# Another opening for a Fourier filter with a two-layer product behind it: where x, the constants and the weights are loaded, and in which order the first steps stand

## The chip, the cores and the metric

The kernel runs on one core of a Trainium2 chip. The metric is the device time of one execution in microseconds (us). Five engines work side by side, each through its own queue of instructions in order: TensorE (PE; its weight loads are listed as PEld), VectorE (DVE), ScalarE (ACT), GpSimd (POOL) and SyncE (SP). DMA transfers are asked for by SP (hardware_dynamic queue q1 in the profile) and by POOL (software_dynamic queue q0); the transfers of both run on the same 16 DMA engines.

## The reference

x has 8 sequences of 3008 tokens with 256 channels, in fp32. Each sequence is filtered by multiplying its Fourier transform with a given complex filter, and each token of the result goes through two matrices with a leaky ReLU between them:

```python
X = np.fft.rfft(x, axis=1)                       # x: (8, 3008, 256)
Y = X * (filt_r + 1j * filt_i)[None, :, :]       # filters: (1505, 256)
y = np.fft.irfft(Y, n=x.shape[1], axis=1).astype(np.float32)
h = y.reshape(24064, 256) @ w_in                 # w_in: (256, 2048)
g = np.maximum(0.01 * h, h)
out = (g @ w_out).astype(np.float32)             # w_out: (2048, 256)
```

## The kernel before

**Tiles and stages.** A sequence is seen as 94 x 32 tokens (N1 = 94 on the partitions, N2 = 32 rows in `x_sb`), and its transform as four small products in fp16. Stage 1 (`s1`) multiplies the 94 side with `fwd1`, a part of `small_sb`. A turn of the data brings the 32 side onto the partitions. Stage 2 (`s2`) multiplies each of 24 columns with its own constant matrix in `f2_sb`; the result is multiplied with the filter in `fa_sb`. Stage `sa` (`inv2r`, `inv2i`) goes back along the 32 side, a second turn follows, and stage `sb` multiplies with `i1_sb` and leaves the filtered sequence in `yt`. From `yt` the two-layer part takes chunks of 512 tokens, 47 of them: `moe1` (L511) multiplies with `w_in_sb`, ACT applies the leaky ReLU (L516), and the second product uses `w_out_sb`, plainly in the first three chunks (L636) and by Strassen's seven products from the fourth on (L575).

**The first sequence** has a way of its own, since nothing can hide it: its turns are DVE transposes (`t1`, `t2`, four each; 0 and 1 belong to the first half of the channels, 2 and 3 to the second) between the buffers `big[0]`, `big[1]` and `big[2]`, not trips through DRAM. The order in which its steps are issued is written out by hand in the string FIRST. Each word calls a function that issues instructions to one engine, and each engine takes its instructions in that order:

- `s1p n0 n b`: PE, stage 1 for rows n0 to n0+n of x into PSUM bank b; `s1e n0 n e`: its eviction by ACT (A) or DVE (D).
- `s2p half c n i b`: PE, stage 2 for n columns from c, i = 0 or 1 for two forms of the constant; `s2d`: DVE multiplies the result with the filter; `s2a` and `s2m`: ACT copies it out of PSUM, four columns at a time, and POOL multiplies it.
- `sap half c b`: PE, stage `sa`, which needs both products of its four columns; `sae`: its eviction by ACT.
- `sbp dt h b`: PE, stage `sb` for half dt of the channels and block h of 376 tokens; `sbe`: its eviction to `yt`. The first chunk of `moe1` needs blocks 0 and 1 of both halves.
- `warm n`: n matmuls on PE with no use for their result.
- `x`, `w_out` (POOL), `f2`, `i1` (SP, each behind a tiny memset on DVE): loads that are issued at that place. `x` loads the second sequence into `x_sb`.
- `xc n0 n e`: rounds rows of x that were loaded in fp32 to fp16.

Ahead of FIRST the first loads are issued: by SP `small_sb` and six of the 32 rows of x in fp32 into the later `big[1]`; by POOL, which casts to fp16 on the way, the other rows in parts of 10, 10 and 6, the first third of `f2_sb`, eight loads of the filters (two half channels, real and imaginary, each in two loads) and `w_in_sb`. POOL's issues wait for earlier ones: the ninth is issued when the first has landed, the tenth when the second has.

**After FIRST** everything is ordered by a planner: each step has a due time in slots (8 to a chunk), and PE alternates between `moe1`, the second product and the stages of the next sequence. Stage 1 of the second sequence (L250) starts in the first chunk, one group of two rows of x after the other; groups 0 to 7 use the first half of `x_sb`, groups 8 to 15 the second. The last stores go out by SP and ACT both.

Of the kernel before, what the change touches and what calls it, by code (L numbers as in the profile page):

```python
# [11 lines left out]
P = 128  # L12
FP16 = mybir.dt.float16
FP32 = mybir.dt.float32
# [5 lines left out]
N1, N2 = 94, 32  # L20
NC = 24
Q = 32
R1 = 96
FP = 3
# [51 lines left out]
def kernel(  # L76
# [9 lines left out]
    nc = tc.nc  # L86
    B, N, D = x.shape
# [33 lines left out]
    f2_d = nc.inline_tensor(f2_np, name="fwd2_const")  # L121
# [6 lines left out]
    f2_sb = cpool.tile([P, NC, P], FP16, name="f2_sb")  # L128
# [5 lines left out]
    w_out_sb = cpool.tile([P, NCT, D], FP16, name="w_out_sb")  # L134
    wt_sb = cpool.tile([P, 4, NCH, P], FP16, name="wt_sb")
    x_sb = cpool.tile([P, N2, D], FP16, name="x_sb")
    big = [cpool.tile([P, Q * D], FP16, name=f"big{i}") for i in range(3)]
# [50 lines left out]
    def x_load(b, n0=0, nn=N2, d0=0, dn=D):  # L188

        for lo, cnt in ((0, R1),) if b + 1 < B else ((0, 64), (64, N1 - 64)):  # L190
            nc.gpsimd.dma_start(
                x_sb[lo : lo + cnt, ds(n0, nn), ds(d0, dn)],
                bass.AP(tensor=x.tensor, offset=x.offset + (b * N + lo * N2 + n0) * D + d0,
                        ap=[[N2 * D, cnt], [D, nn], [1, dn]]))

    def filt_load(lo, src, d0, dn):

        for q, first, sgn in ((lo, 0, 1), (lo + Q, N1, -1)):
            nc.gpsimd.dma_start(
                fa_sb[q : q + Q, :, ds(d0, dn)],  # L200
                bass.AP(tensor=src.tensor, offset=src.offset + first * D + d0,
                        ap=[[N1 * D, N2 // 2], [sgn * NC * D, 2], [sgn * D, NC], [1, dn]]))

    EARLY = 6
    x_early = big[1][:].bitcast(FP32)[:, : EARLY * D].rearrange("p (n d) -> p n d", n=EARLY)
    nc.sync.dma_start(small_sb[:], small_d.ap())
    nc.sync.dma_start(x_early[:R1], bass.AP(tensor=x.tensor, offset=x.offset, ap=[[N2 * D, R1], [D, EARLY], [1, D]]))
    for n0, nn in ((6, 10), (16, 10), (26, 6)):  # L210
        x_load(0, n0, nn)
    nc.gpsimd.dma_start(f2_sb[:, : NC // FP, :], f2_d.ap()[0])
    for hf in range(2):

        filt_load(0, filt_r, hf * DH, DH)
        filt_load(64, filt_i, hf * DH, DH)
    nc.gpsimd.dma_start(w_in_sb[:], moe_w_in.rearrange("(dt p) c -> p dt c", p=P))
    idle = cpool.tile([P, CH], FP16, name="idle")
    nc.vector.memset(idle[:], 0.0)
# [136 lines left out]
    engine = {"A": act, "D": dve}  # L356
# [91 lines left out]
        nc.vector.memset(i1_sb[:, 0, 0:2], 0.0)  # L448
        nc.sync.dma_start(i1_sb[:], i1_d.ap())

    def load_f2():
        nc.vector.memset(f2_sb[:, NC // FP, 0:2], 0.0)
        nc.sync.dma_start(f2_sb[:, NC // FP :, :].rearrange("p (i c) m -> p i (c m)", i=FP - 1),
                          f2_d.ap()[1:].rearrange("i p c m -> p i (c m)"))

    def load_x(half):
        x_load(1, half * N2 // 2, N2 // 2)
        issued.add(("x", 1, 0))

    def load_w_out():  # L460
        nc.gpsimd.dma_start(w_out_sb[:], moe_w_out.rearrange("(ct p) d -> p ct d", p=P))

    def round_x(n0, n, e):
        engine[e](x_sb[:N1, ds(n0, n), :], x_early[:N1, ds(n0, n), :])

    FIRST = """
        xc 0 4 A, xc 4 2 D, warm 18, s1p 0 0 4 b3, s1p 0 4 2 b0, warm 3, s1p 0 14 2 b1, s1e 0 4 2 D,
        s1e 0 0 4 A, s1p 0 10 4 b4, s1e 0 10 4 A, s1p 0 6 4 b3, s1e 0 14 2 D, warm 4, s1p 0 20 4 b4,
        s1e 0 6 4 D, s1p 0 16 4 b3, s1e 0 16 4 A, s1p 0 26 2 b2, s1p 0 24 2 b0, s1e 0 24 2 A, f2, s1e 0 20 4 D,
        s1p 0 28 2 b1, s1p 0 30 2 b4, s1e 0 26 2 D, s1e 0 30 2 A, s1e 0 28 2 D, t1 0, t1 1, warm 14,  # L470
        s2p 0 0 4 0 b3, s2p 0 0 4 1 b2, warm 2, s2p 0 8 4 1 b0, s2a 0 0 4 0, s2a 0 0 4 1, t1 3,
        s2p 0 12 4 1 b4, t1 2, s2d 0 8 4 1, s2p 0 12 4 0 b1, s2p 0 16 8 0 b3, x 0, x 1, s2m 0 0 4 0,
        s2m 0 0 4 1, s2d 0 16 8 0, s2a 0 12 4 1, s2p 0 8 4 0 b2, s2p 1 16 8 0 b4, s2p 0 4 4 1 b0, s2a 0 12 4 0,
        s2d 0 8 4 0, s2a 1 16 8 0, s2p 0 4 4 0 b1, s2p 1 16 8 1 b3, s2d 0 4 4 0, s2a 1 20 8 0, sap 0 8 b2,
        s2d 0 4 4 1, s2a 1 16 8 1, s2a 1 20 8 1, s2m 0 12 4 0, s2p 0 16 8 1 b4, sap 0 0 b1, s2p 1 0 8 1 b3,
        s2m 0 12 4 1, sap 0 12 b0, s2m 1 20 8 0, sae 0 8 A, s2d 0 16 8 1, sae 0 0 A, s2p 1 8 8 1 b4,
        sap 0 4 b2, i1, s2d 1 0 8 1, sap 0 16 b1, sae 0 12 A, s2p 1 8 8 0 b3, sap 0 20 b0, s2d 1 8 8 1,
        s2m 1 20 8 1, sae 0 4 A, s2d 1 8 8 0, s2p 1 0 8 0 b4, sae 0 16 A, sap 1 20 b2, s2d 1 0 8 0,
        sap 1 12 b1, sae 0 20 A, sap 1 8 b0, s2m 1 16 8 0, sae 1 20 A, s2m 1 16 8 1, w_out, sae 1 12 A,
        sae 1 8 A, sap 1 16 b3, sae 1 16 A, sap 1 4 b2, t2 1, sae 1 4 A, sap 1 0 b4, t2 0, sae 1 0 A, warm 4,  # L480
        sbp 0 1 b1, sbp 0 4 b0, sbp 0 0 b3, sbp 0 3 b2, t2 3, sbe 0 1 A, sbe 0 4 A, sbe 0 0 A, sbp 0 2 b4,
        sbp 0 7 b1, sbp 0 6 b0, t2 2, sbe 0 2 A, sbe 0 7 A, sbp 0 5 b3, sbp 1 0 b4, sbp 1 1 b1, sbe 0 6 A,
        sbe 0 5 A, sbe 1 1 A, sbe 0 3 D, sbe 1 0 D
    """
    steps = dict(s1p=s1p, s1e=s1e, t1=t1, s2p=s2p, s2d=s2d, s2a=s2a, s2m=s2m, sap=sap, sae=sae, t2=t2,
                 sbp=sbp, sbe=sbe, i1=load_i1, f2=load_f2, x=load_x, w_out=load_w_out,
                 xc=round_x, warm=keep_warm)
    for step in FIRST.split(","):
        what, *args = step.split()
        steps[what](*(int(v) if v.isdigit() else v for v in args))  # L490
# [184 lines left out]
    for b in range(1, B):  # L675
        z = 47 * (b - 4) if b > 4 else 0
        p = PLANS[min(b, 4) - 1]
# [18 lines left out]
    while queue:  # L696
        time, n, stage, b, g, f = heapq.heappop(queue)
# [62 lines left out]
```

## Time and profile before

| | |
|---|---|
| time, median of 3 runs (lowest, highest) | 756.67 us (755.65, 757.60) |
| the profiled execution | 756.67 us, of which the span from first to last instruction is 754.9 |
| PE busy | 738.9 us, 98% of the span |
| DVE, ACT, POOL busy | 67%, 74%, 22% |
| DMA | 113.64 MB, mean 151 GB/s |
| granted PE clock, mean | 0.996 |

The page lists busy times of the engines, the span in 40 slices, the DMA queues, the chain of work that ended last, and the costliest groups of instructions. Rows of the timeline have start, length, engine, line, operation, what is written and read, and in brackets how long the engine had been idle and who ended that. Times count from the first instruction. Sizes in DMA views are those of the data as written: x counts half of what is read.

### The profile page before, as it was taken

Reading aid. Unit: us, or ns where it says so; the run is one execution under the profiler, and the core shown is the slowest. Engines: PE = TensorE matmul, PEld = TensorE weight load, DVE = VectorE, ACT = ScalarE, POOL = GpSimd, SP = SyncE. Lnnn points to the kernel's source line nnn. Section 1 sums busy time; section 2 is a strip of 40 time slices with the busy share of each in tenths; the row PEclk is TensorE's granted clock in tenths of the full one; section 3 lists DMA queues with packets and bytes.
Section 4 is the critical chain, followed back from the end, with each engine's and each line's share of the span. In section 5 each row is a group of like instructions: output and inputs, shape, how many; then the busy total and the mean of one; then the engine's idle time right before and its main releaser. Section 6 shows DMA issues by size and latency. Waiting matters only on the chain.

```text
span 754.9 us, 19393 instructions
## 1 busy us (share of the span) xinstructions
PE 738.9 (98%) x8017; PEld 529.2 (70%) x8017; DVE 502.2 (67%) x686; ACT 559.8 (74%) x755; POOL 166.5 (22%) x168
## 2 busy tenths in 40 slices
PE   8799999999999999999999999999999999999997
PEld 3446667776777777877778777787777777777775
DVE  5777555677776776667667766776677676465565
ACT  4675787888887787787778777877777777777662
POOL 5502430332222222222233222212212210000000
PEclk9999999999999999999999999999999999999999
DMA  9996798887876567565676566444554333111011
GB/s 203 227 199 164 176 215 219 212 187 197 223 194 162 135 188 211 140 155 144 178 191 164 142 183 168 137 141 120 140 164 122 106 101 104 57 54 54 29 51 63
DMA packets 119672, 113.64 MB, mean 151 GB/s; under 512 B 16336, under 2 KB 92752, under 8 KB 119392
## 3 DMA queue, kind: packets, MB, share of 16 engines
q1 hardware_dynamic: 104543, 95.95, 43.2%
q0 software_dynamic: 14752, 16.19, 15.7%
q8 instruction: 62, 1.02, 0.6%
q10 hardware_dynamic: 289, 0.26, 0.1%
q14 instruction: 26, 0.21, 0.1%
HBM read 57.51 MB, written 50.33 MB: 143 GB/s over the span
## 4 chain that ended last, share of the span: by engine, by line
PE 91%; DMA 5%; DVE 2%; ACT 1%; POOL 1%; issue 0%; SPq 0%; DVEq 0%; ACTq 0%
PE ph L511 41%; PE po_ps L575 18%; PE pf L575 18%; PE pf L250 3%; PE pf L342 3%; PE pf L321 2%; PE pf L299 2%; DMA i_sb<-inv_const 1%; PE po_ps L636 1%; PE pf L636 1%; DMA f_sb<-fwd_const 1%; DMA dz<-big 1%; DMA big<-in_x_dram 1%; POOL y_b_g L314 1%; DMA p_b_g<-p_b_g 1%; PE pf L433 0%
## 5 line engine op out<-in xcount | busy, mean ns | idle before, releaser
L516 ACT ACTIVATE gt_c<-ph 128x1024 f16<-128x1024 f32 x376 | 385.7, 1026 | 135.2 <-PE ph L511 124.5
L511 PE MATMUL ph<-yt,w_in_sb 128*128 128x512 f16 (+7 forms) x1728 | 447.3, 351 | 0.2
L575 PEld LDWEIGHTS <-gt_c 128*128 128x128 f16 x2800 | 202.2, 98 | 91.2 <-issue 0.2
L314 POOL TENSOR_TENSOR y_b_g<-p_b_g,p_b_g 128x512 f16<-128x512 f32 x84 | 118.8, 1416 | 416.4 <-DMA p_b_g<-p_b_g 198.2
L575 PEld LDWEIGHTS <-big 128*128 128x128 f16 x2128 | 151.2, 98 | 61.6 <-issue 0.2
L511 PEld LDWEIGHTS <-w_in_sb 128*128 128x128 f16 x1728 | 137.5, 98 | 20.9 <-issue 1.5
L308 DVE TENSOR_TENSOR p_b_g<-pf,fb_sb 128x512 f32<-128x512 f32 x78 | 53.7, 688 | 32.6 <-PE pf L299 14.7
L575 PE MATMUL po_ps<-wt_sb,gt_c 128*128 128x128 f16 x704 | 70.0, 219 | 0.0
L575 PE MATMUL pf<-wt_sb,gt_c 128*128 128x128 f16 x688 | 68.4, 219 | 0.0
L575 PE MATMUL pf<-w_out_sb,gt_c 128*128 128x128 f16 x720 | 67.9, 219 | 0.0
L332 ACT CAST yt<-pf 128x376 f16<-128x376 f32 x120 | 56.3, 471 | 15.5 <-PE pf L342 8.0
L575 PE MATMUL po_ps<-wt_sb,big 128*128 128x128 f16 x720 | 67.4, 219 | 0.1
L575 PE MATMUL pf<-wt_sb,big 128*128 128x128 f16 x704 | 67.2, 219 | 0.0
L253 ACT CAST big<-pf 128x512 f16<-128x512 f32 x100 | 58.2, 588 | 11.9 <-PE pf L250 10.1
L575 PE MATMUL po_ps<-w_out_sb,gt_c 128*128 128x128 f16 x688 | 66.0, 219 | 0.0
L311 DVE TENSOR_TENSOR p_b_g<-pf,fa_sb 128x512 f32<-128x512 f32 x84 | 57.2, 682 | 1.4 <-POOL y_b_g L314 1.3
L548 DVE TENSOR_TENSOR big<-gt_c 128x2048 f16<-128x2048 f16 (+1 forms) x46 | 57.5, 1250 | 0.1
L548 DVE TENSOR_TENSOR gt_c<-gt_c 128x2048 f16<-128x2048 f16 x43 | 55.5, 1291 | 1.0
L548 DVE TENSOR_TENSOR big<-gt_c,big 128x2048 f16<-128x2048 f16 (+1 forms) x45 | 55.2, 1226 | 0.0
L548 DVE TENSOR_TENSOR big<-big,gt_c 128x2048 f16<-128x2048 f16 (+1 forms) x45 | 55.0, 1222 | 0.1
L323 ACT CAST big<-pf 128x512 f16<-128x512 f32 x84 | 49.0, 584 | 5.8 <-PE pf L321 4.0
L250 PE MATMUL pf<-x_sb,small_sb 94*128 94x512 f16 x112 | 42.7, 381 | 0.9 <-DVE big L253 0.9
(88 smaller groups left out, 619.7 us busy)
## 6 DMA issues: line engine op xcount, KB each, us to landing
dz<-big SPq DMA_DIRECT2D x98, 256.0 KB
p_b_g<-p_b_g SPq DMA_DIRECT2D x156, 128.0 KB
out_dram<-ost_c_h SPq DMA_DIRECT2D x119, 128.0 KB
big<-dz SPq DMA_DIRECT2D x42, 256.0 KB
big<-dz SPq DMA_DIRECT2D x56, 192.0 KB
x_sb<-in_x_dram POOLq DMA_DIRECT2D x40, 192.0 KB, 4.5
x_sb<-in_x_dram POOLq DMA_DIRECT2D x2, 768.0 KB, 18.8
w_in_sb<-in_moe_w_in_dram POOLq DMA_DIRECT2D x1, 1024.0 KB, 13.4
```

The lines of the kernel that those rows point to most:

```text
L250: nc.tensor.matmul(ps, fwd1[:N1], x_sb[:N1, ds(2 * g, 2), :], start=True, stop=True)
L253: copy(st[:, ds(2 * (g % 2), 2), :], ps)
L308: nc.vector.tensor_tensor(p2[:], ps, fb, AL.mult)
L311: nc.vector.tensor_tensor(p1[:], ps, fa, AL.mult)
L314: ("y", b, g), lambda: nc.gpsimd.tensor_tensor(y1[:], p1[:], p3[:], AL.add)))
L323: nc.scalar.copy(st2[h % 4][:, ds(2 * (g % 2), 2), :], ps)
L332: copy(yv, ps.rearrange("p c a -> p a c"))
L342: nc.tensor.matmul(ps[:, j, :], z2[h % 4][:K4, j, ts(dt, P)], i1_sb[:K4, 4 * h + j, :], start=True, stop=True)
L511: nc.tensor.matmul(ph[:, j, ds(t - ci * CH, e - t)], w_in_sb[:, dt, ts(ct, P)], yt[:, dt, ds(t % N, e - t)], start=(dt == 0), stop=(dt == ...
L516: nc.scalar.activation(gts[ci][:, ds(2 * g, 2), :], ph, AF.Lrelu)
L548: nc.vector.tensor_tensor(*(v[:, ds(c0, n)] for v in (o, i0, i1)), op)
L575: nc.tensor.matmul(po[:, t], a()[:, c, ts(t, P)], w[:, c, :], start=(c == 0), stop=(c == NCH - 1))
```

## The change

All rows of the first sequence of x are loaded by POOL's queue with the cast, in parts of 10, 10, 8 and 4; the fp32 load and the rounding steps `xc` are gone. The thirds of `f2_sb` are all loaded ahead of FIRST: the second and the first by SP right after `small_sb`, the last by POOL between the two halves of the filters; the step `f2` is gone. `x` now issues one half of the second sequence, `w_out_sb` and the other half, all three together on POOL; `w_out` is no step of its own. FIRST is another order of the same kinds of steps: `i1` comes earlier, `x` later, among POOL's products; the split of products between DVE and POOL, the PSUM banks and the warm matmuls differ in places.

```diff
--- before.py
+++ after.py
@@ -202,18 +202,18 @@
                         ap=[[N1 * D, N2 // 2], [sgn * NC * D, 2], [sgn * D, NC], [1, dn]]))
 
 
-
-    EARLY = 6
-    x_early = big[1][:].bitcast(FP32)[:, : EARLY * D].rearrange("p (n d) -> p n d", n=EARLY)
     nc.sync.dma_start(small_sb[:], small_d.ap())
-    nc.sync.dma_start(x_early[:R1], bass.AP(tensor=x.tensor, offset=x.offset, ap=[[N2 * D, R1], [D, EARLY], [1, D]]))
-    for n0, nn in ((6, 10), (16, 10), (26, 6)):
+    for i in (1, 0):
+        nc.sync.dma_start(f2_sb[:, ts(i, NC // FP), :], f2_d.ap()[i])
+    first_parts = ((0, 10), (10, 10), (20, 8), (28, 4))
+    for n0, nn in first_parts:
         x_load(0, n0, nn)
-    nc.gpsimd.dma_start(f2_sb[:, : NC // FP, :], f2_d.ap()[0])
     for hf in range(2):
 
         filt_load(0, filt_r, hf * DH, DH)
         filt_load(64, filt_i, hf * DH, DH)
+        if hf == 0:
+            nc.gpsimd.dma_start(f2_sb[:, ts(2, NC // FP), :], f2_d.ap()[2])
     nc.gpsimd.dma_start(w_in_sb[:], moe_w_in.rearrange("(dt p) c -> p dt c", p=P))
     idle = cpool.tile([P, CH], FP16, name="idle")
     nc.vector.memset(idle[:], 0.0)
@@ -448,43 +448,34 @@
         nc.vector.memset(i1_sb[:, 0, 0:2], 0.0)
         nc.sync.dma_start(i1_sb[:], i1_d.ap())
 
-    def load_f2():
-        nc.vector.memset(f2_sb[:, NC // FP, 0:2], 0.0)
-        nc.sync.dma_start(f2_sb[:, NC // FP :, :].rearrange("p (i c) m -> p i (c m)", i=FP - 1),
-                          f2_d.ap()[1:].rearrange("i p c m -> p i (c m)"))
-
-    def load_x(half):
-        x_load(1, half * N2 // 2, N2 // 2)
+    def load_x():
+
+        x_load(1, 0, N2 // 2)
+        nc.gpsimd.dma_start(w_out_sb[:], moe_w_out.rearrange("(ct p) d -> p ct d", p=P))
+        x_load(1, N2 // 2, N2 // 2)
         issued.add(("x", 1, 0))
 
-    def load_w_out():
-        nc.gpsimd.dma_start(w_out_sb[:], moe_w_out.rearrange("(ct p) d -> p ct d", p=P))
-
-    def round_x(n0, n, e):
-        engine[e](x_sb[:N1, ds(n0, n), :], x_early[:N1, ds(n0, n), :])
-
     FIRST = """
-        xc 0 4 A, xc 4 2 D, warm 18, s1p 0 0 4 b3, s1p 0 4 2 b0, warm 3, s1p 0 14 2 b1, s1e 0 4 2 D,
-        s1e 0 0 4 A, s1p 0 10 4 b4, s1e 0 10 4 A, s1p 0 6 4 b3, s1e 0 14 2 D, warm 4, s1p 0 20 4 b4,
-        s1e 0 6 4 D, s1p 0 16 4 b3, s1e 0 16 4 A, s1p 0 26 2 b2, s1p 0 24 2 b0, s1e 0 24 2 A, f2, s1e 0 20 4 D,
-        s1p 0 28 2 b1, s1p 0 30 2 b4, s1e 0 26 2 D, s1e 0 30 2 A, s1e 0 28 2 D, t1 0, t1 1, warm 14,
-        s2p 0 0 4 0 b3, s2p 0 0 4 1 b2, warm 2, s2p 0 8 4 1 b0, s2a 0 0 4 0, s2a 0 0 4 1, t1 3,
-        s2p 0 12 4 1 b4, t1 2, s2d 0 8 4 1, s2p 0 12 4 0 b1, s2p 0 16 8 0 b3, x 0, x 1, s2m 0 0 4 0,
-        s2m 0 0 4 1, s2d 0 16 8 0, s2a 0 12 4 1, s2p 0 8 4 0 b2, s2p 1 16 8 0 b4, s2p 0 4 4 1 b0, s2a 0 12 4 0,
-        s2d 0 8 4 0, s2a 1 16 8 0, s2p 0 4 4 0 b1, s2p 1 16 8 1 b3, s2d 0 4 4 0, s2a 1 20 8 0, sap 0 8 b2,
-        s2d 0 4 4 1, s2a 1 16 8 1, s2a 1 20 8 1, s2m 0 12 4 0, s2p 0 16 8 1 b4, sap 0 0 b1, s2p 1 0 8 1 b3,
-        s2m 0 12 4 1, sap 0 12 b0, s2m 1 20 8 0, sae 0 8 A, s2d 0 16 8 1, sae 0 0 A, s2p 1 8 8 1 b4,
-        sap 0 4 b2, i1, s2d 1 0 8 1, sap 0 16 b1, sae 0 12 A, s2p 1 8 8 0 b3, sap 0 20 b0, s2d 1 8 8 1,
-        s2m 1 20 8 1, sae 0 4 A, s2d 1 8 8 0, s2p 1 0 8 0 b4, sae 0 16 A, sap 1 20 b2, s2d 1 0 8 0,
-        sap 1 12 b1, sae 0 20 A, sap 1 8 b0, s2m 1 16 8 0, sae 1 20 A, s2m 1 16 8 1, w_out, sae 1 12 A,
-        sae 1 8 A, sap 1 16 b3, sae 1 16 A, sap 1 4 b2, t2 1, sae 1 4 A, sap 1 0 b4, t2 0, sae 1 0 A, warm 4,
-        sbp 0 1 b1, sbp 0 4 b0, sbp 0 0 b3, sbp 0 3 b2, t2 3, sbe 0 1 A, sbe 0 4 A, sbe 0 0 A, sbp 0 2 b4,
-        sbp 0 7 b1, sbp 0 6 b0, t2 2, sbe 0 2 A, sbe 0 7 A, sbp 0 5 b3, sbp 1 0 b4, sbp 1 1 b1, sbe 0 6 A,
-        sbe 0 5 A, sbe 1 1 A, sbe 0 3 D, sbe 1 0 D
+        warm 18, s1p 0 0 2 b0, s1e 0 0 2 A, s1p 0 2 4 b3, s1p 0 6 4 b4, s1e 0 2 4 D, warm 4, s1p 0 16 4 b3,
+        s1e 0 16 4 D, s1p 0 10 2 b1, s1e 0 6 4 A, s1p 0 12 4 b4, s1e 0 10 2 A, warm 2, s1p 0 24 2 b2,
+        s1e 0 12 4 A, s1e 0 24 2 D, s1p 0 20 4 b3, s1e 0 20 4 A, s1p 0 26 2 b0, s1p 0 28 2 b1,
+        s1p 0 30 2 b2, s1e 0 26 2 D, s1e 0 28 2 A, s1e 0 30 2 D, t1 1, t1 0, warm 14, s2p 0 0 4 0 b0,
+        s2p 0 0 4 1 b1, s2p 0 16 4 0 b2, t1 2, t1 3, s2a 0 0 4 0, s2m 0 0 4 0, s2a 0 0 4 1, s2p 0 16 4 1 b0,
+        s2p 0 8 8 0 b4, s2p 0 8 8 1 b3, s2a 0 16 4 0, s2m 0 16 4 0, s2a 0 16 4 1, s2m 0 16 4 1,
+        s2p 0 4 4 0 b1, s2d 0 8 8 0, s2p 0 20 4 1 b2, s2d 0 8 8 1, i1, s2d 0 4 4 0, s2p 0 4 4 1 b0,
+        s2p 1 8 8 0 b4, s2d 0 4 4 1, warm 1, s2p 1 8 8 1 b3, s2a 1 8 8 0, s2m 0 0 4 1, sap 0 8 b1,
+        s2a 1 12 8 0, s2p 1 16 8 0 b4, s2d 0 20 4 1, sap 0 16 b0, s2m 1 12 8 0, x, s2a 1 8 8 1, s2m 1 8 8 1,
+        s2d 1 16 8 0, sae 0 8 A, s2a 1 12 8 1, sae 0 16 A, s2p 0 20 4 0 b2, sap 0 4 b1, s2m 1 12 8 1,
+        s2p 1 16 8 1 b3, sap 0 0 b0, s2p 1 0 8 1 b4, s2d 0 20 4 0, s2d 1 16 8 1, sae 0 4 A, s2m 1 8 8 0,
+        sae 0 0 A, sap 0 20 b1, s2d 1 0 8 1, sap 0 12 b2, s2p 1 0 8 0 b3, sap 1 16 b0, sae 0 20 A,
+        sae 0 12 A, sap 1 12 b1, s2d 1 0 8 0, sap 1 20 b2, t2 0, sap 1 8 b4, t2 1, sae 1 16 A, sap 1 4 b0,
+        sap 1 0 b3, sae 1 12 A, warm 5, sbp 0 1 b1, sae 1 20 A, sae 1 8 A, sbp 0 4 b2, sae 1 4 A, sae 1 0 A,
+        t2 3, sbp 0 5 b4, sbe 0 1 A, sbp 0 2 b0, t2 2, sbe 0 4 A, sbp 0 6 b3, sbe 0 5 A, sbp 0 7 b1,
+        sbp 0 0 b2, sbp 0 3 b4, sbe 0 6 A, sbp 1 1 b3, sbe 0 0 D, sbe 0 2 A, sbp 1 0 b0, sbe 0 3 A,
+        sbe 0 7 A, sbe 1 1 D, sbe 1 0 A
     """
     steps = dict(s1p=s1p, s1e=s1e, t1=t1, s2p=s2p, s2d=s2d, s2a=s2a, s2m=s2m, sap=sap, sae=sae, t2=t2,
-                 sbp=sbp, sbe=sbe, i1=load_i1, f2=load_f2, x=load_x, w_out=load_w_out,
-                 xc=round_x, warm=keep_warm)
+                 sbp=sbp, sbe=sbe, i1=load_i1, x=load_x, warm=keep_warm)
     for step in FIRST.split(","):
         what, *args = step.split()
         steps[what](*(int(v) if v.isdigit() else v for v in args))
```

## The prediction

> **What bounds the kernel now.** I read the page first, then the chain of waits of the opening, then the timelines of POOL and SP with the rates of the transfers.
>
> The sums of three stretches say where a gain could lie. Columns: stretch, its length, busy time of PE, PEld, DVE, ACT, POOL with counts, granted PE clock, DMA share, GB/s.
>
> ```profile
> 0.00:40.00 40.00, 32.56 (x312) 17.49 (x313) 26.57 (x32) 21.02 (x36) 20.11 (x28) 0.96 1.20 215
> 40.00:740.00 700.00, 697.04 (x7561) 503.24 (x7559) 467.36 (x639) 536.51 (x717) 146.40 (x140) 1.00 0.57 149
> ```
>
> From 40 us on PE has no slack to speak of (3 us in 700), and the diff touches nothing there. All of the change lies in the opening, before the first product with `w_in_sb` (L511). Whatever moves that start moves the end by as much, as long as PE then waits for nothing new. So the question is: when does L511 start? The chain of waits of the opening (start, length, what):
>
> ```profile
> 1.18 5.24 DMA big<-in_x_dram
> ...
> 11.46 6.98 DMA f_sb<-fwd_const
> ...
> 24.48 11.09 DMA i_sb<-inv_const
> 35.58 0.14 issue
> 35.71 0.85 PE pf L433 x16
> ...
> 37.54 2.05 ACT yt L332 x5
> 39.59 0.04 issue
> 39.63 0.81 PE ph L511 x3
> ```
>
> The last delay is the load of `i1_sb`: issued at 24.48, used at 35.71. The work it joins was ready earlier: the list of waits has
>
> ```profile
> PE pf L433 <- DMA i_sb<-inv_const: 4.5, 1, 4.5
> ```
>
> and on DVE the four transposes `t2` run from 29.06 to 33.78, the first two, which are all that the first `sbp` needs, to about 31.45. So 4.2 us of the opening hang on this one load. Why it takes 11 us is seen in the queues:
>
> ```profile
> 14.49 0.72 POOL L217 DMA_DIRECT2D w_in_sb<-in_moe_w_in_dram  x1
> 15.63 0.55 POOL L191 DMA_DIRECT2D x_sb<-in_x_dram  x1 [0.41 <-issue]
> 17.09 0.52 POOL L191 DMA_DIRECT2D x_sb<-in_x_dram  x1 [0.91 <-PE ph L388]
> 18.76 9.00 POOL L396 TENSOR_TENSOR prod<-spare,fa_sb 128x512 f16<-128x512 f32 x8 [1.14 <-DMA fa_sb<-in_filt_i_dram]
> 27.71 1.23 POOL L461 DMA_DIRECT2D w_out_sb<-in_moe_w_out_dram  x1
> ```
>
> POOL asks for both halves of the next sequence at 15.6 and 17.1, long before SP asks for `i1_sb`. The DMA engines are full (share 1.0 and more in every stretch from 6 to 34.6), so the load shares them with 1.5 MB that nobody needs yet.
>
> **Prices.** Filter halves move at 178 GB/s (12 to 15 us), so one load of 197 KB takes 1.1 us. Parts of x move at 208 (6 to 10 us): 492 KB take 2.4, 393 KB 1.9, 197 KB 0.95, a third of `f2` (262 KB) 1.3. `w_in` moves at 214 (23 to 26 us): 4.9 us. Mixed traffic of `i1_sb` and x ran at 269 (27.9 to 34.6), `w_out` at 193 (36 to 41). On the engines: `t1`, `t2` 1.18 each; a 4-column filter product 1.125 on POOL, 0.65 on DVE (8 columns 1.2); an ACT copy 0.5; `sap` 0.44; a warm matmul 0.215.
>
> **Part 1: the start.** Removed: the 590 KB fp32 load and its two casts (1.05 on ACT, 0.42 on DVE, both before 7.5). Six rows of x move to POOL's queue. In the first 4.2 us that queue delivered nothing (only queue 1 shows packets). On SP the two early thirds of `f2` (524 KB) take the place of the 590 KB; they fit into the same stretch, and no PE step needs them before 16.9, so I cost them at nothing; without that cover they would delay x by 524/208 = 2.5. Before, the first 10-row part was in by 8.50 (POOL's next issue waits for it), the second by 10.82, 2.3 later, as priced. Without the rest of the fp32 load beside it I put the first part at 7.9 (bounds: 4.2+2.4+0.7 = 7.3, and 8.5 as before), then 10.3, 12.2 and 13.1 for the last part, against at most 12.35 before. Only two 2-row evictions follow the last part, so `t1` starts at 14.5, not 14.21: a loss of 0.3.
>
> The Trainium skill, "SBUF — State Buffer", section on the shared port pair, speaks against this part: VectorE in a two-port mode keeps GpSimd from writing descriptors, so loads asked for by GpSimd starve where SP's do not. The trace has a DVE memset from 1.34 to 2.25 just there and the first POOL packets only after 4.2, which fits but is no proof. By the rule the x parts would again start no earlier than 4.2, which is the number used.
>
> **Part 2: the thirds of `f2`.** The wait of 0.53 on PE at 18.49 for the late two thirds goes, and so do DVE's memset and SP's issue at 11.46. What is late next is the last third, now behind x and half the filters: 13.1 + 4x1.1 + 1.3 = 18.8. The new order asks for it third (`s2p 0 16 4 0`), so PE stands there from 17.5 to 18.8; behind it are the products that DVE and POOL wait for. The second half of the filters lands at 18.8+4.4 = 23.2, as now; POOL's fifth product wants it at 23.15.
>
> **Part 3: POOL.** POOL's second product starts with that third, at 19.8. Its next three follow without a gap: 19.8+4x1.125 = 24.3. Then `x` issues three loads there: 0.55+1.23+0.52 = 2.3, plus a 0.4 gap as the row at 15.63 has: 27.0. Before, two of them stood at 15.6 to 17.6, ahead of the first product; behind them now stand POOL's last three products, which PE's last `sap`s wait for: 27.0+3.4 = 30.4. Then three `sap` (1.3) and five warm matmuls (1.1): the first `sbp` can start at 32.8. DVE's `t2 0, t2 1` end at 31.9 and hide behind that. Walking the old order with these prices gives an `sbp` ready at 31.5 without the load, and L511 at 39.5 where the trace has 39.63.
>
> **Part 4: `i1_sb`.** Its place is now behind DVE's second 8-column product, 22.3. SP's two loads under full engines had 7.0 (`f2`) and 11.1 us (`i1_sb`) from issue to use: it lands between 29.3 and 33.4. Most of it now runs beside `w_in`, and x is asked for only at 24.3 or later, so I take 9.5, between the two: 31.8. That is under 32.8, so it costs nothing in the forecast, 0.6 at the late end.
>
> **Sum.** The first `sbp` moves from 35.71 to 32.8: -2.9. Behind it both orders have eight evictions on ACT and two on DVE before L511 (3.9 us from 35.71 to 39.63), so L511 moves to 36.7. The profiled execution took 756.67 us with a span of 754.9; it is the median of the three runs itself. 756.67-2.9 = 753.8.
>
> Clock: the row
>
> ```profile
> 36.00:38.00 2.00, 2.00 (x59) 2.00 (x55) 0.55 (x1) 1.69 (x5) 0.00 (x0) 0.50 1.38 190
> ```
>
> shows half the clock after the 4.45 us wait. ACT's evictions set the pace there (0.41 each), so I count no gain from a full clock; at most 0.3. The Trainium skill, "TensorE: Matmul & The Clock Gate", Part 1, puts the halving at about 3.4 us of idleness; by it the new order, whose longest gap is some 1.3 us, would keep the clock.
>
> **Rivals.** *The load waits again.* `i1_sb` still shares the engines with x, and lands 11.1 to 13.3 us after 22.3 (13.3 if the first half of x, 0.79 MB at 269 GB/s, delays it by most of 2.9 us more): 33.4 to 35.6. The time is 754.4 to 756.6. For it: this is what the trace shows once. Against: x is issued 2 us after it, not 9 us before.
>
> *The third of `f2` is late.* Each us past 18.8 goes through POOL to the first `sbp`. With all filters ahead of it (23.2) the gain would be gone; a slip of 1.5 gives 755.3. Against: POOL asks for it ninth, before the second half of the filters, and nothing else is in that queue.
>
> *Slower: the next sequence is late.* Its second half now stands behind `w_out`. By the prices: 23.2, `w_in` 4.9, `i1_sb` and the first half 1.56 MB/269 = 5.8, `w_out` 5.4, second half 3.6: 42.9, in by 43.5. The ninth group of L250 wants it at 47.60-2.9 = 44.7 and holds PE with all of L511 behind it. If the stores of the first groups (1.05 MB) and the reload of `f2` (0.79 MB) get ahead of it at 210 GB/s, it is in 8.8 later, at 52.3: PE stands 7.6, and the time is 756.67-2.9+7.6 = 761.4. It turns the sign from a landing at 47.6 on, when nearly half of that traffic goes first. For it: the margin is only 1.2. Against: from 41 to 44 us the engines were half free (share 0.56, 37 GB/s).
>
> *The change is not what its words say.* Read-backs at 2.2 slots, the products and the stores by two queues are in the kernel already (READ, W0, `stores`), so nothing is to be had from them.
>
> **How the numbers follow.** A change within 0.3% (2.3 us: 754.4 to 758.9) is about what a measurement of this kernel cannot tell from none. The forecast has 0.62, its own range 752.6 (x 0.6 and POOL 0.3 earlier: -3.8, and 0.3 for a full clock) to 755.2 (the third or the load 1.4 late): 0.52 of it faster, 0.10 within. The waiting load has 0.18, of which 0.02 faster and 0.16 within; the late third 0.05, within; the late next sequence 0.15, slower. That makes 0.54, 0.31 and 0.15. The range runs from 752.5 to 757.0 and leaves out the slower case and little else.
>
> **What would show it.** Right: L433's first wait for `i_sb` under 1 us, first L433 near 32.8, L511 near 36.7, the clock at 1.00 from 36 to 38, POOL's three issues between 24 and 27, PE waiting for `f_sb` at about 18, the first L250 near 37.5 and the ninth near 44.7 without a DMA wait. Wrong: a wait for `x_sb` at the ninth L250, `i1_sb` in after 34, the last part of x after 14, or idle PE beyond 40 us that the profile of before does not have.

## The result and the profile after

The new kernel takes 753.76 us (median of 4 runs, 753.22 to 754.33) against 756.43 for the old one beside it (4 runs, 755.65 to 757.60). The ratio is 0.9964, with a 95% interval of 0.9946 to 0.9981: 2.7 us or 0.36% faster. The profiled execution took 754.03 us, its span is 752.2, 2.7 below the old one.

The same two stretches as before (stretch, its length, busy time of PE, PEld, DVE, ACT, POOL, granted PE clock, DMA share, GB/s):

```profile
0.00:40.00 40.00, 35.98 (x326) 18.73 (x327) 27.70 (x33) 22.80 (x39) 21.56 (x31) 1.00 1.23 210
40.00:740.00 700.00, 696.20 (x7580) 503.81 (x7579) 465.81 (x640) 535.85 (x716) 142.07 (x139) 1.00 0.56 148
```

PE works 3.4 us more within the first 40 us, as it gets to the common work sooner; in the 700 us behind it is busy for 0.8 us less than before (696.2 against 697.0), which is taken up at the end. The chain of waits of the opening no longer holds any DMA in its last part (start, length, what):

```profile
24.60 0.59 POOL x_sb L191
25.20 1.17 POOL w_out_sb L454
26.37 0.53 POOL x_sb L191
...
26.91 3.40 POOL prod L396 x3
...
32.64 2.38 DVE big L425 x2
...
35.07 0.47 PE ph L433 x6
...
35.63 0.56 DVE yt L332
...
36.23 1.03 PE ph L502 x4
```

What decides now is POOL: its three issues of loads, then its last three products, then, by way of PE's last `sap`s and their evictions on ACT, the second pair of transposes `t2` on DVE. L502 is the L511 of the old kernel. The load of `i1_sb`, its first use, and the place where PE stands instead, from the timelines of SP and PE:

```profile
22.68 0.32 SPq L449 DMA_DIRECT2D i_sb<-inv_const  x1
```
```profile
18.91 0.40 PE L388 MATMUL pf<-big,f_sb 128*128 128x128 f16 x4 [1.06 <-DMA f_sb<-fwd_const]
...
32.82 0.69 PE L433 MATMUL pf<-i_sb,big 128*64 128x94 f16 x16
...
44.37 0.39 PE L250 MATMUL pf<-x_sb,small_sb 94*128 94x512 f16 x1
```

The first `sbp` has no wait in brackets: the load was in at 31.87 by the trace's completion records, 9.2 us after its issue instead of 11.1. The wait for the last third of `f2` is there, 1.06 us long. The last row is the ninth group of L250, which has no DMA wait either; the second half of the next sequence was in at 42.0.

### The profile page after: what moved, and what is told of

Its sections match the earlier page's. It is cut to its first block, busy times and chain, and to the rows that moved or that the text cites. A ratio compares the mean times of both kernels' runs of the same rounds, so it can differ in the third digit from the quotient of the medians.

```text
span 752.2 us, 19384 instructions
## 1 busy us (share of the span) xinstructions
PE 738.8 (98%) x8016; PEld 528.9 (70%) x8016; DVE 499.3 (66%) x683; ACT 559.0 (74%) x755; POOL 163.6 (22%) x169
## 4 chain that ended last, share of the span: by engine, by line
PE 91%; DMA 2%; DVE 2%; POOL 1%; ACT 0%; issue 0%; SPq 0%; DVEq 0%; ACTq 0%
PE ph L502 42%; PE po_ps L566 18%; PE pf L566 18%; PE pf L250 3%; PE pf L342 3%; PE pf L321 2%; PE pf L299 2%; PE po_ps L627 1%; PE pf L627 1%; DMA dz<-big 1%; DMA p_b_g<-p_b_g 1%; POOL prod L396 0%; DMA big<-dz 0%; POOL y_b_g L314 0%; DVE big L425 0%
## 5 line engine op out<-in xcount | busy, mean ns | idle before, releaser
L502 PE MATMUL ph<-yt,w_in_sb 128*128 128x512 f16 (+7 forms) x1728 | 447.2, 351 | 0.5 <-DVE yt L332 0.5
L314 POOL TENSOR_TENSOR y_b_g<-p_b_g,p_b_g 128x512 f16<-128x512 f32 x84 | 115.4, 1374 | 418.8 <-DMA p_b_g<-p_b_g 245.4
L502 PEld LDWEIGHTS <-w_in_sb 128*128 128x128 f16 x1728 | 137.5, 98 | 20.9 <-issue 1.8
L250 PE MATMUL pf<-x_sb,small_sb 94*128 94x512 f16 x112 | 42.7, 381 | 0.8 <-DVE big L253 0.8
```

What stands on the lines that cost most here:

```text
L250: nc.tensor.matmul(ps, fwd1[:N1], x_sb[:N1, ds(2 * g, 2), :], start=True, stop=True)
L314: ("y", b, g), lambda: nc.gpsimd.tensor_tensor(y1[:], p1[:], p3[:], AL.add)))
L502: nc.tensor.matmul(ph[:, j, ds(t - ci * CH, e - t)], w_in_sb[:, dt, ts(ct, P)], yt[:, dt, ds(t % N, e - t)], start=(dt == 0), stop=(dt == ...
```

## Experiments

Two readings of why `i1_sb` had been so late stood against each other (A and B in the expectations), with a third (C) that the gain came from elsewhere. "Old" and "new" are the two kernels of the result; the median of the old one beside these runs was 756.59 (first four), 756.61 (next four) and 756.27 (last two).

Each kernel has one profile, and single steps vary from one execution to the next: in the seven profiles with the new loads ahead of FIRST, the first part of x is in between 7.15 and 8.26 us. A difference of half a microsecond between two profiles is therefore no effect by itself.

### The load alone, in the old kernel

`i1` earlier:

```diff
-        ... s2p 0 16 8 0 b3, x 0, x 1, s2m 0 0 4 0, s2m 0 0 4 1, s2d 0 16 8 0, s2a 0 12 4 1, ...
+        ... s2p 0 16 8 0 b3, x 0, x 1, s2m 0 0 4 0, s2m 0 0 4 1, s2d 0 16 8 0, i1, s2a 0 12 4 1, ...
-        ... sap 0 4 b2, i1, s2d 1 0 8 1, ...
+        ... sap 0 4 b2, s2d 1 0 8 1, ...
```

> The old kernel with one word of FIRST moved: i1 is issued behind the DVE product s2d 0 16 8 0 (about 21.2 us) instead of 24.5. Theory A (POOL's loads stand in one queue behind w_in whatever is done, so what counts is how early i1_sb is asked for and whether its packets run beside w_in or beside x): it lands 9 to 9.5 us after its issue, by 30.7, the first sbp waits for the transposes instead (31.5), and the time falls by 4.0 to 752.4. Theory B (the halves of x asked for at 15.6 and 17.1 crowd it, so the 11.1 us from issue to use stay): it lands at 32.3, -3.3, 753.1. Theory C (the gain of the change came from the wait for f2 and from the clock): less than 1 us.

Measured: 752.27 us, ratio 0.9949 (0.9937 to 0.9962). The issue and the first `sbp`:

```profile
21.26 0.34 SPq L449 DMA_DIRECT2D i_sb<-inv_const  x1
```
```profile
31.54 0.69 PE L433 MATMUL pf<-i_sb,big 128*64 128x94 f16 x16 [0.21 <-DVE big L425]
```

The load was in at 30.5, 9.2 after its issue, as A said and not B. The first `sbp` waits for DVE's transposes.

x later:

```diff
-        ... s2p 0 16 8 0 b3, x 0, x 1, s2m 0 0 4 0, ...
+        ... s2p 0 16 8 0 b3, s2m 0 0 4 0, ...
-        ... s2m 1 16 8 1, w_out, sae 1 12 A, ...
+        ... s2m 1 16 8 1, x 0, x 1, w_out, sae 1 12 A, ...
```

> The old kernel with the two loads of the second sequence moved behind POOL's last product (27.7 instead of 15.6 and 17.1), ahead of w_out; i1 stays where it was (24.5). Theory A: the queue has w_in until 27.6 either way and only stands empty for 1 to 1.5 us, so i1_sb (first packets at 27.9) gets the engines alone for that long and lands at 33 to 34 instead of 35.6: -1.6 to -2.6. Theory B: without x ahead of it it lands 7 to 9.5 us after its issue, at 31.5 to 34: -1.6 to -4.1.

Measured: 751.79 us, ratio 0.9945 (0.9933 to 0.9957). The rows of SP and PE:

```profile
24.51 0.34 SPq L449 DMA_DIRECT2D i_sb<-inv_const  x1
```
```profile
31.50 0.69 PE L433 MATMUL pf<-i_sb,big 128*64 128x94 f16 x16 [0.21 <-DVE big L425]
```

Issued at the same time as in the old kernel, the load was in at 30.5: 6.0 us instead of 11.1. So the 1.5 MB of x, asked for early and needed by nobody, cost this load 5 us. That is B, and more than A's queue behind `w_in` allows (33 at the earliest). The first `sbp` now waits for DVE's transposes, as the prediction read off the old trace: 31.5.

Both moves together:

> The old kernel with both moves. Both theories: i1_sb lands before 31.5 and the first sbp waits for the transposes, -4.0, 752.4; by A no better than i1 early alone, by B better than it by 0.7.

Measured: 751.88 us, ratio 0.9939 (0.9926 to 0.9951), first `sbp` at 31.46. The three kernels agree within their spread. Either move is enough, since the transposes are next. B is right about the crowding. A is right that an earlier issue shortens the load too, because more of it then runs beside `w_in`; by B alone the first of the three would have kept its 11.1.

How the crowding works is seen in what the two queues moved in 2 us in which the load (all that q1 has there) was under way. These are the packets, MB and share of the 16 engines in the old kernel (28 to 30 us, x beside the load), in the old kernel with `i1` early (26 to 28, the end of `w_in` and the first of x beside it) and in the new kernel (26 to 28, the end of `w_in` beside it and no x yet):

```profile
q0 software_dynamic: 35, 0.29, 68.3%
q1 hardware_dynamic: 43, 0.26, 32.5%
```
```profile
q0 software_dynamic: 64, 0.24, 59.4%
q1 hardware_dynamic: 63, 0.38, 47.3%
```
```profile
q1 hardware_dynamic: 119, 0.69, 83.3%
q0 software_dynamic: 33, 0.09, 22.5%
```

As long as POOL's queue has enough to do, both queues move about as many packets (35 and 43, 64 and 63), as if they took turns. By the trace's packet records the load's packets have 6016 bytes, those of x 8192 and those of `w_in` 4096, so the load gets less beside x than beside `w_in`. It gets most where `w_in` runs out and x has not come yet.

### The clock

```diff
-        ... sae 1 0 A, warm 4, ...
+        ... sae 1 0 A, warm 24, ...
```

> The old kernel with 24 warm matmuls instead of 4 ahead of the first sbp, so that PE is not idle while it waits for i1_sb and the granted clock stays at 1.00 from 36 to 38 us. Theories A and B: the evictions set the pace there, so 0 to -0.3 (756.1 to 756.4). Theory C: the half clock is a good part of the 2.7, so -1 or more.

Measured: 757.23 us, ratio 1.0015 (1.0005 to 1.0024). The row for 36 to 38 us, PE's list of waits, the first `sbp` and the first activation:

```profile
36.00:38.00 2.00, 1.95 (x63) 1.98 (x65) 0.55 (x1) 1.47 (x5) 0.00 (x0) 1.00 1.41 196
```
```profile
PE pf L433 <- DMA i_sb<-inv_const: 0.9, 1, 0.9
```
```profile
36.05 0.69 PE L433 MATMUL pf<-i_sb,big 128*64 128x94 f16 x16 [0.85 <-DMA i_sb<-inv_const]
```
```profile
40.59 1.02 ACT L516 ACTIVATE gt_c<-ph 128x1024 f16<-128x1024 f32 x1 [0.96 <-PE ph L511]
```

And the first activation of the old kernel, whose first `sbp` is at 35.71:

```profile
40.53 1.02 ACT L516 ACTIVATE gt_c<-ph 128x1024 f16<-128x1024 f32 x1 [0.96 <-PE ph L511]
```

The clock is 1.00 where the old kernel had 0.50, the load is as late as ever (11.8 us after its issue, in at 35.9; PE's wait is short only because warm matmuls fill it), and the time does not fall. C, which wanted 1 us or more, falls. The half clock did have a price of its own, though a small one: from the first `sbp` to the first activation it is 4.54 us here and 4.82 in the old kernel. The other nine profiles whose clock stayed at 1.00 there have 4.53 to 4.56 in eight cases and 4.71 in one. Here the 0.3 is hidden, as the load came 0.3 later.

### The same load in the new kernel

`i1` three DVE products later, `i1` where it was but x asked for early, and x asked for last:

```diff
# i1 late
-        ... s2d 0 8 8 1, i1, s2d 0 4 4 0, ...
+        ... s2d 0 8 8 1, s2d 0 4 4 0, ...
-        ... s2d 1 16 8 0, sae 0 8 A, s2a 1 12 8 1, ...
+        ... s2d 1 16 8 0, i1, sae 0 8 A, s2a 1 12 8 1, ...
# x early
-        ... t1 2, t1 3, s2a 0 0 4 0, s2m 0 0 4 0, ... s2m 1 12 8 0, x, s2a 1 8 8 1, ...
+        ... t1 2, t1 3, x, s2a 0 0 4 0, s2m 0 0 4 0, ... s2m 1 12 8 0, s2a 1 8 8 1, ...
# x last
-        ... s2m 1 12 8 0, x, s2a 1 8 8 1, ... s2m 1 8 8 0, sae 0 0 A, ...
+        ... s2m 1 12 8 0, s2a 1 8 8 1, ... s2m 1 8 8 0, x, sae 0 0 A, ...
```

> The new kernel with i1 moved three DVE products later, behind s2d 1 16 8 0 (issue at about 25.7 instead of 22.7). Theory A: its packets start at about 28.9, all beside those of x, and it lands at 36.4: the first sbp moves from 32.8 to 36.4 and the whole gain is gone, 757.4. Theory B: x is still asked for no earlier than 24.6, so the 9.2 us from issue to landing stay: 34.9, +2.1, 755.9. Theory C (f2 and the clock): below +1.

Measured: 755.56 us, ratio to the old kernel 0.9986 (0.9977 to 0.9994), 1.8 above the new one. Issue at 24.7, in at 33.3, that is 8.5 later. PE's row:

```profile
33.39 0.68 PE L433 MATMUL pf<-i_sb,big 128*64 128x94 f16 x16 [1.46 <-DMA i_sb<-inv_const]
```

8.5 is less than either theory had, and it does not decide between them, since neither's condition was met. POOL was 0.8 ahead of the new kernel's profile in this execution (its second product at 19.2 instead of 20.0), so x was asked for at 23.6, ahead of the load and not behind it; and the load's packets did not all run beside x. From 30 us on POOL's queue was mostly at `w_out`, whose packets have 512 bytes, and in 30 to 32 us the load got twice what it got beside x:

```profile
q1 hardware_dynamic: 98, 0.54, 67.3%
q0 software_dynamic: 112, 0.10, 29.0%
```

PE waited 1.46 for the load again, and all eleven runs are slower than the slowest of the new kernel. With this one word moved, 1.0 us of the gain is left, so in the new kernel, too, most of it hangs on this load. The two profiles differ by less than the medians (first `sbp` at 33.39 against 32.82), as the rest of the path was early in this execution.

> The new kernel with the word x (half of the second sequence, w_out, other half) moved ahead of POOL's first product, to about 16 us instead of 24.6. Theory A (one queue behind w_in, so asking earlier changes nothing in the order of the data): i1_sb lands at 31.9 as in the new kernel, POOL's last three products come 2.3 earlier, and the first sbp waits for i1_sb or the transposes at 32.1 instead of 32.8: -0.5 to -0.7 against the new kernel. Theory B (x asked for ahead of i1 crowds it): it lands 11.1 after its issue at 33.8, +1.0 against the new kernel.

Measured: 753.78 us, ratio 0.9965 (0.9953 to 0.9977). The load took 10.4 us (21.5 to 31.9), 1.2 more than in the new kernel: the crowding is there again. It happened to be asked for 1.2 earlier, since in this execution the third of `f2` came earlier, so it landed when A said, for another reason. POOL's products came early, as forecast, PE waited 1.0 for `i1_sb`, and L502 stood at 35.32 in the profile, 0.9 before the new kernel's. The profiled execution is the fastest of the six; the medians are the same.

> The new kernel with the word x moved behind POOL's last product. Both theories: the 2.3 us of issues leave the path of the last three products; what is late next is DVE, whose transposes t2 0 and 1 end at 32.1, so the gain is 0.5 to 0.6, not 2.3. i1_sb lands at 31 or earlier. The second half of x lands near 44 and may hold the ninth group of L250 (43.8) by a few tenths.

Measured: 753.98 us, ratio 0.9962 (0.9948 to 0.9976), runs from 752.12 to 756.50. In the profile L502 is at 35.48, 0.75 earlier, so the 2.3 us of issues were worth little more than the 0.6 that was forecast: DVE is next. PE's list of waits has the forecast wait at L250:

```profile
PE pf L250 <- DMA x_sb<-in_x_dram: 0.7, 1, 0.7
```

The median shows none of the gain; with runs 4 us apart, a difference of 0.5 can't be seen here, and these two runs are inconclusive on the time.

### The start and the third of `f2`

The new loads ahead of FIRST with the old order, first alone, then with x late as above:

```diff
-    nc.sync.dma_start(x_early[:R1], ...)
-    for n0, nn in ((6, 10), (16, 10), (26, 6)):
+    for i in (1, 0):
+        nc.sync.dma_start(f2_sb[:, ts(i, NC // FP), :], f2_d.ap()[i])
+    for n0, nn in ((0, 10), (10, 10), (20, 8), (28, 4)):
         x_load(0, n0, nn)
...
-        xc 0 4 A, xc 4 2 D, warm 18, ... s1e 0 24 2 A, f2, s1e 0 20 4 D, ...
+        warm 18, ... s1e 0 24 2 A, s1e 0 20 4 D, ...
```

> The old kernel with the new loads ahead of FIRST alone: x all by POOL in parts of 10, 10, 8 and 4, two thirds of f2 by SP at the start, the last by POOL; the fp32 load, the roundings and the step f2 are gone, the rest of FIRST is the old one. Theories A and B: the first sbp still waits for i1_sb at about 35.6, so nothing is seen, -0.3 to +0.3. Theory C: the wait for f2 goes, -0.5 to -1.

Measured: 757.67 us, ratio 1.0017 (1.0009 to 1.0026): about 1.1 slower, where A and B expected nothing. The rows of DVE and SP show why:

```profile
15.77 4.63 DVE L380 STREAM_TRANSPOSE big<-big 128x1024 f32<-128x1024 f32 x4 [0.28 <-ACT big L280]
...
25.38 0.06 DVE L449 MEMSET i_sb<- 128x1 uint32 x1
```
```profile
25.48 0.32 SPq L450 DMA_DIRECT2D i_sb<-inv_const  x1
```

The old order of stage 1, written for rows that come early, puts off the transposes from 14.2 to 15.8. The word `i1` stands in DVE's queue behind them, so the load that everything waits for is asked for 1.0 later and is in at 36.1. Both expectations left out that a late DVE is a late `i1`. This is half of the loss: the first `sbp` is at 36.25, 0.54 after the old kernel's. The other half is the clock, which stayed at 0.50 from 36 to 40 us and at 0.60 from 40 to 42, while the old kernel's was back at 1.00 from 40 on: from the first `sbp` to the first activation it is 5.45 us here instead of 4.82.

> The new loads ahead of FIRST with the old order (as in the kernel where only these were taken over) and, besides, the two loads of the second sequence behind POOL's last product. With i1_sb out of the way the price of the new start alone is seen. Theory B: the transposes t1 start 1.5 later than in the old kernel and the chain behind them is 1.0 later, so the first sbp is at 32.5 and the time about 1.0 above that of the old kernel with x late (752.8). Rival (the new start costs 0.3 as in the sum of the prediction, the rest of the loss with it was the later i1): 752.1.

Measured: 752.29 us, ratio 0.9953 (0.9934 to 0.9971), first `sbp` at 31.96 against 31.50 without the new loads. The price of the new start with the old order is 0.5 at the first `sbp`, between the two forecasts. The medians differ by as much (751.79 with x late alone), but their intervals overlap; `t1` started 1.1 late here, not 1.5, since the first part of x came 0.4 earlier in this execution.

Last, the third of `f2` ahead of all filters, in the new kernel:

```diff
+    nc.gpsimd.dma_start(f2_sb[:, ts(2, NC // FP), :], f2_d.ap()[2])
     for hf in range(2):
         filt_load(0, filt_r, hf * DH, DH)
         filt_load(64, filt_i, hf * DH, DH)
-        if hf == 0:
-            nc.gpsimd.dma_start(f2_sb[:, ts(2, NC // FP), :], f2_d.ap()[2])
```

> The new kernel with the last third of f2 issued by POOL ahead of all filters instead of between their halves. PE's wait of 1.1 us at 18.9 goes; the first half of the filters lands 1.3 later. If the third is a step of the path as the prediction has it (each us it is earlier is a us, through POOL's second product): up to -1.1 against the new kernel. Rival (POOL's products then wait for the filters at 18.9 to 20.0 instead, so that the path only changes its name): within 0.3 of the new kernel.

Measured: 752.30 us, ratio 0.9951 (0.9932 to 0.9970). The median is 1.5 below the new kernel's, but the two intervals overlap. The wait for `f_sb` is gone, POOL's second product follows the first without a gap, and the first `sbp` comes 1.3 earlier than at 32.82:

```profile
31.52 0.69 PE L432 MATMUL pf<-i_sb,big 128*64 128x94 f16 x16
```

About 0.5 of this comes from x, whose parts landed earlier in this execution; the remaining 0.8 is the wait. It was long in the new kernel's profile, though: the three variants above that load `f2` in the same order waited 0.25 to 0.28 for the third, not 1.06. So the new kernel leaves something where the prediction said it would, 0.3 to 1.1 us by the profiles, and the runs do not fix it more closely.

## Why the prediction was right

**By its steps.** Forecast and measured, in us: the first part of x in at 7.9 and 7.79; the transposes `t1` from 14.5 and 14.68; the third of `f2` at 18.8 and 18.9; POOL's second product at 19.8 and 20.0; its three issues from 24.3 to 27.0 and 24.6 to 26.9; the end of its last products at 30.4 and 30.3; `i1_sb` asked for at 22.3 and 22.7, in at 31.8 and 31.9; the first `sbp` at 32.8 and 32.82. The wait for the load went, and POOL's moved issues took back a part of the 4.2 us, as the sum had it. That the steps agree to 0.1 or 0.2 is partly luck: in other profiles with the new loads ahead of FIRST, x's first part was in as early as 7.15 and as late as 8.26, and the third of `f2` as early as 17.7.

**Why the load was late.** The prediction's reason, that x was asked for long before and nobody needed it, held: 11.1 us with x ahead, 6.0 without. It named only half of it: asking 3 us earlier with x still ahead shortens it to 9.2. In the new kernel 0.69 of the load's 0.77 MB came from 26 to 28 us, beside the end of `w_in` and ahead of x, as Part 4 had it.

**Right for the wrong reason.** Part 1 cost the early thirds of `f2` at nothing because they would fit ahead of x, which would begin at 4.2. They didn't. By the DMA view of 4.2 to 8.9 us both queues ran (packets, MB, share of the 16 engines):

```profile
q0 software_dynamic: 174, 0.80, 86.0%
q1 hardware_dynamic: 137, 0.25, 15.7%
```

A quarter of a megabyte of `f2` stood in x's way, 1.2 us by the prediction's price of 208 GB/s. POOL's queue, for its part, did not wait for 4.2: its first packets came at 3.2, with the DVE memset that the prediction pointed to at the same place (1.34 to 2.25), and 0.15 MB were in before 4.2. The two errors about cancel. Why x began earlier than in the old kernel is open.

**Mis-sized.** The step behind the first `sbp` was kept at its old 3.9 us, with nothing for the full clock. The 39.63 of the old chain is where L511's second product starts; its first is at 39.19, which makes 3.5, and in the new kernel it is 3.4 (32.82 to 36.23). To the first activation, the same point in both, it is 4.82 before and 4.53 after:

```profile
37.35 1.02 ACT L507 ACTIVATE gt_c<-ph 128x1024 f16<-128x1024 f32 x1 [0.94 <-PE ph L502]
```

The 0.3 between them is the clock's price, as the experiment with 24 warm matmuls has it, and the "at most 0.3" that the prediction left out. The gain was thus 2.9 at the first `sbp`, 3.2 by the first activation. That the time came out at the forecast all the same is luck: 1.0 was lost again at 115 us, in PE's list of waits of the new kernel:

```profile
PE pf L342 <- DMA big<-dz: 1.2, 1, 1.2
```

The old profile has 0.2 there; the differences of the activations' starts show the loss (3.20 before, 2.22 after it) and 0.4 that comes back by 230 us. This wait for a read-back was 0.2 to 1.5 in six of the ten experiments' profiles and absent in the other four, with L511 early or late, so it changes from one execution to the next; what sets it is open.

**The rivals.** The load that waits again did not happen in the new kernel, but one word moved brings it back (755.56). The third of `f2` was on time and still on the path (a wait of 1.06 in this profile). The next sequence was in 2.4 us before its use, not 1.2; with x last it was 0.7 late, so that rival was near. The clock stayed at 1.00, which fits the rule of the Trainium skill, "TensorE: Matmul & The Clock Gate", Part 1 (no gap of PE between its first matmul and L502 was longer than 1.1 us); it was worth the 0.3 above.

**A better kernel.** The old kernel with x asked for behind POOL's last product beats both: 751.79, 0.9945 of the old one, with a single move of two words; all five of its runs are below all four of the new kernel's (highest 753.09, lowest 753.22). The gain of the change was the load of `i1_sb`; its new start, its late third and POOL's issues gave back 1.3 us at the first `sbp` (32.82 against 31.50).

## What to carry to other kernels

A load that ends a stage late is not always asked for late: look at what else the DMA engines carry at that time and who needs it when, and put bulk loads for the next stage behind it. When a wait goes, read off the trace what would have been ready next; here that gave the limit (31.5) which three of the variants then reached. An instruction that issues a load, or a memset ahead of one, is as late as its place in its engine's queue, and belongs in the sum with its transfer.

## What the runs showed of the hardware that we had not expected

The time from issue to landing of one load of 0.77 MB on SP's queue was between 4.7 and 11.8 us in these kernels. The four largest values (10.4 to 11.8) came where x stood in POOL's queue ahead of it; the two smallest (6.0 with x late, 4.7 with the new start besides) where x was behind it and `w_in` nearly through. In those two its first packets came 1.7 and 1.2 us after the issue, in the other ten profiles 3.2 to 3.6.

While the load and another transfer were both under way, the two queues moved about the same number of packets, which makes the size of the other's packets set the load's share: 0.26 MB in 2 us beside packets of 8192 bytes, 0.38 beside those of 4096 with some of 8192, 0.54 beside mostly those of 512.

PE at half clock cost 0.3 us where it lasted from 36 to about 39 us: keeping it warm changed the clock from 0.50 to 1.00 and the stretch from the first `sbp` to the first activation from 4.82 to 4.54 us. Where the half clock lasted beyond 40 us that stretch took 5.45.
